# Twenty instead of twenty-three weight pieces converted early, late conversions that end on GpSimd, and a third buffer for q

## The chip, the cores and the metric

The kernel runs on one core of a Trainium2 chip. The metric is the device time of one execution in microseconds (us), lower is better. Three timed runs of the kernel before gave 1148.38, 1149.02 and 1145.77 us (median 1148.38). One further execution was recorded by the hardware profiler.

## The reference

```
# retention, 4 batches, 8 heads, 768 steps, head size 64
state = gamma * state + outer(k[t], v[t]);  y[t] = scale * q[t] @ state
x = y as 3072 tokens of 512
# first mixture: 8 experts, each takes 384 tokens
logits = x @ w_gate; walk all (token, expert) pairs in falling order of logit,
    give a free token to an expert that is not full
out[mask] = relu(x[mask] @ w1[e]) @ w2[e]
# second part, all tokens, width 1536
out = (sigmoid(x @ w_gate2) * (x @ w_val)) @ w_out
```

The three weights of the second part arrive as float64. [...]

## The kernel before

**Stages.** First comes the retention, in 24 iterations of 128 tokens: TensorE transposes q and k (`turn_q`, `turn_k`), multiplies (`stage_a`, `stage_y`), and turns the result back and takes the logits (`stage_x`), whose rows go to DRAM (`xd`). Then the routing of the first expert (`members(0)`), which has little beside it. Then eight experts in turn. An expert has two phases. In the first, `h_step` and `y_step` alternate over 8 blocks of the hidden width. In the second, `g_step` and `o_step` go over 12 blocks of the second part. Each product is made of three matmuls on a high and a low part of both factors: ScalarE rounds the high part (L584), VectorE subtracts to get the low part (L585), six pieces at most ahead of their use.

**Hooks.** Behind each product of an expert stands a hook (`hook()`), numbered from 0 (`units`); the first expert has 51. A hook does two things: it runs the next step of the routing of the following expert (small VectorE instructions, then compares `cm` at L255 and counting matmuls at L264 that read them), and it runs whatever the table `late` has at that number.

**The conversion of a piece.** The 36 pieces (128 rows by 512 numbers) of the three float64 weights end in the tile `wall`. For one piece: a DMA brings `raw`; ScalarE scales the low word (L151); VectorE shifts and masks the high word (L152) and joins sign and top bit (L154); ScalarE takes the absolute value of the high word (L156), GpSimd adds the low word (L157); VectorE multiplies by the test "not smaller than the smallest normal" (L159). Before, 23 pieces are converted in slots of the retention (`conv_at`, two slots per iteration) and 13 in hooks of the first expert (`LATE`, three hooks for each piece: L151, L152 and L154 in hook u, L156 and L157 in u+1, L159 in u+3).

**Order.** The schedule is written by hand: each engine executes its instructions in the order in which the program issues them. SyncE issues nearly all DMAs, in program order too; it waits at a DMA whose buffer is still in use, with everything behind it. GpSimd also scales k in the retention (L277) and issues the indirect gathers and scatters of tokens.

Of the kernel before, what the change touches and what calls it, by code (L numbers as in the profile page):

```python
# [8 lines left out]
F32 = mybir.dt.float32  # L9
# [5 lines left out]
OP = mybir.AluOpType  # L15
# [4 lines left out]
def retention_moe_glu_kernel(  # L20
# [15 lines left out]
    PE, ACT, DVE, POOL, SP = nc.tensor, nc.scalar, nc.vector, nc.gpsimd, nc.sync  # L36
    B, H, S, D = q.shape
    C = S // 128
    NCH = B * C
# [20 lines left out]
    loads = attn.enter_context(tc.tile_pool(name="loads", bufs=5))  # L60
# [6 lines left out]
    tq, tk, tv = {}, {}, {}  # L67

    def load_q(j):
        b, g = divmod(j, C // 2)  # L70
        tq[j] = loads.tile([128, H, 2, D], F32, name="q", bufs=2)
        SP.dma_start(tq[j].rearrange("p h r d -> p h (r d)"),
                     q[b, :, g * 256:(g + 1) * 256, :].rearrange("h (p r) d -> p h (r d)", r=2))

    def load_k(i):
        b, c = divmod(i, C)
        tk[i] = loads.tile([128, H, D], F32, name="k", bufs=6)
        SP.dma_start(tk[i], k[b, :, c * 128:(c + 1) * 128, :].rearrange("h t d -> t h d"))

    def load_v(i):  # L80
        b, c = divmod(i, C)
        tv[i] = loads.tile([128, H, D], F32, name="v", bufs=5)
        SP.dma_start(tv[i], v[b, :, c * 128:(c + 1) * 128, :].rearrange("h t d -> t h d"))
# [9 lines left out]
    load_k(0)  # L93
    load_k(1)
    load_q(1)
    load_v(0)
    load_k(2)
# [28 lines left out]
    SMALLEST = 1.125 * 2.0 ** -15  # L126
# [18 lines left out]
    def conv_steps(m):  # L145

        t = raws.pop(m)
        lo, hi = t[:, :, 0], t[:, :, 1]
        w = wall[:, seq[m]].rearrange("p a b -> p (a b)")
        wi = w.bitcast(I32)  # L150
        ACT.activation(lo, lo.bitcast(U32), AF.Copy, scale=2.0 ** -29)  # L151
        DVE.tensor_scalar(wi, hi, 3, 0x3FFFFFFF, op0=OP.logical_shift_left, op1=OP.bitwise_and)  # L152
        yield
        DVE.scalar_tensor_tensor(wi, hi, -1073741824, wi, op0=OP.bitwise_and, op1=OP.bitwise_or)  # L154
        yield
        ACT.activation(hi.bitcast(F32), hi.bitcast(F32), AF.Abs)  # L156
        POOL.tensor_tensor(wi, wi, lo, OP.add)  # L157
        yield
        DVE.scalar_tensor_tensor(w, hi.bitcast(F32), SMALLEST, w, op0=OP.is_ge, op1=OP.mult)  # L159

    steps = {}

# [106 lines left out]
    def scale_q(j):  # L269
        raw = tq[j]  # L270
        tq[j] = work.tile([128, 2, H, D], F32, name="qs", bufs=2)
        for r in range(2):
            DVE.tensor_tensor(tq[j][:, r], raw[:, :, r, :],
                              dq[:, j % (C // 2), r, :, None].to_broadcast([128, H, D]), OP.mult)

    def scale_k(i):
        POOL.tensor_tensor(tk[i], tk[i], dk[:, i % C, :, None].to_broadcast([128, H, D]), OP.mult)  # L277

    def turn_q(u):
        j, z = divmod(u, 2)  # L280
        if z == 0:
            qT[j] = work.tile([128, HP, 256], F32, name="qT", bufs=3)
        p = psa.tile([128, 2, 128, 2], F32, name="pT", bufs=2)
        for a in range(2):
            for r in range(2):
                h = 4 * z + 2 * a
                PE.transpose(p[:, a, :, r], tq[j][:, r, h:h + 2, :], ident)
        ACT.activation(qT[j][:, 2 * z:2 * z + 2, :], p.rearrange("p a i r -> p a (i r)"), AF.Copy)

    def turn_k(i):  # L290
        p = psa.tile([128, HP, 128], F32, name="pT", bufs=2)
        for a in range(HP):
            PE.transpose(p[:, a, :], tk[i][:, 2 * a:2 * a + 2, :], ident)
        kT[i] = work.tile([128, HP, 128], F32, name="kT", bufs=3)
        ACT.activation(kT[i], p, AF.Copy)
# [4 lines left out]
    def stage_a(i):  # L300
        am = work.tile([128, 2, HP, 128], F32, name="am", bufs=2)
        ps = [psa.tile([128, HP, 128], F32, name=f"pA{s}") for s in range(2)]
        for a in range(HP):
            for s in range(2):
                r = slice(s * 64, (s + 1) * 64)
                PE.matmul(ps[s][:, a, :], kT[i][r, a, :], q_of(i)[r, a, :], start=True, stop=True)  # L306
        for s in range(2):
            DVE.tensor_tensor(am[:, s], ps[s], mask_b, OP.mult)
        AM[i] = am

    def stage_y(i):
        c = i % C
        pY = psa.tile([128, HP, 128], F32, name="pY")

        if c:
            for a in range(HP):
                PE.matmul(pY[:, a, :], Sbd[c % 2][:, a, :], q_of(i)[:, a, :], start=(a == 0), stop=False,  # L317
                          skip_group_check=True)
        for a in range(HP):
            for s in range(2):  # L320
                PE.matmul(pY[s * 64:(s + 1) * 64, a, :], tv[i][:, 2 * a + s, :], AM[i][:, s, a, :],  # L321
                          start=(not c and a == 0), stop=True, skip_group_check=True)
        t = work.tile([128, HP, 128], F32, name="xT", bufs=2)
        ACT.activation(t, pY, AF.Copy)
        XT[i] = t
        if c < C - 1:
            for a in range(HP):
                PE.matmul(pS[:, a, :], tk[i][:, 2 * a:2 * a + 2, :], tv[i][:, 2 * a:2 * a + 2, :],  # L328
                          start=(c == 0 and a == 0), stop=(c == C - 2), skip_group_check=True)
            sn = Sbd[(c + 1) % 2]  # L330
            for s in range(2):
                r = slice(s * 64, (s + 1) * 64)
                ACT.activation(sn[r, :, r], pS[r, :, r], AF.Copy)

    def stage_x(i):
        xs = work.tile([128, HP, 128 + E], F32, name="xs", bufs=3)
        for z in range(2):
            p = psa.tile([128, 2, 128 + E], F32, name=f"pX{z}")
            for a in range(2):
                PE.matmul(p[:, a, :], XT[i][:, 2 * z + a, :], eyew[:, 2 * z + a, :], start=True, stop=True)  # L340
            if z:
                ACT.activation(xs[:, 2:, :], p, AF.Copy)
            else:
                DVE.tensor_copy(xs[:, :2, :], p)
        SP.dma_start(xd[i * 128:(i + 1) * 128, :].rearrange("p (a b) -> p a b", a=HP), xs[:, :, :128])
        XS[i] = xs
# [21 lines left out]
        DVE.tensor_reduce(lg[:, i, :], XS[i][:, :, 128:].rearrange("p a e -> p e a"), AX, OP.add)  # L368


    EARLY = 23
    LATE = [1 + 5 * n // 2 for n in range(NP - EARLY)]
    RAWS = 3
    conv_at = {4 + n * 41 // EARLY: n for n in range(EARLY)}

    def conv_slot(u):
        if u + 3 in conv_at:
            conv_load(conv_at[u + 3], conv, 5)
        if u in conv_at:
            conv_step(conv_at[u], 2)  # L380
        if u - 1 in conv_at:
            conv_step(conv_at[u - 1])
        if u - 3 in conv_at:
            conv_step(conv_at[u - 3])

    for i in range(NCH):
        if i + 5 < NCH:
            load_k(i + 5)
        if i + 4 < NCH:
            load_v(i + 4)  # L390
        if i % 2 == 0 and i // 2 + 3 < NCH // 2:
            load_q(i // 2 + 3)
        if i % 2 == 0 and i // 2 + 2 < NCH // 2:
            scale_q(i // 2 + 2)
        if i + 3 < NCH:
            scale_k(i + 3)
        if i + 2 < NCH:
            turn_k(i + 2)
        if i + 3 < NCH:
            turn_q(i + 3)  # L400
        if i + 1 < NCH:
            stage_a(i + 1)
        conv_slot(2 * i)
        stage_y(i)
        if i:
            stage_x(i - 1)
        if i >= 2:
            reduce_x(i - 2)
        conv_slot(2 * i + 1)
        if i == 1:  # L410
            late_consts()
        if i == NCH - 4:
            prep_tiles()
            prep(0, 10, True)
        if i == NCH - 3:
            begun = [compare(0, 0, 10, 1 << widths[0], r["edb"], OP.is_le)]
        if i == NCH - 2:
            prep(10, 20, True)
            begun.append(compare(1, 10, 20, 1 << widths[0], r["edb"], OP.is_le))
# [9 lines left out]
    main = ctx.enter_context(tc.tile_pool(name="main", bufs=1))  # L429
# [30 lines left out]
    def fetch_tokens(x):  # L460
# [11 lines left out]
        if x == 0:  # L472
            for n in range(RAWS):
                conv_load(EARLY + n, main, RAWS)

# [275 lines left out]
    late = {}  # L751
    for n, u in enumerate(LATE):
        m = EARLY + n
        if n + RAWS < len(LATE):
            late.setdefault(u + 4, []).append((conv_load, m + RAWS, main, RAWS))
        late.setdefault(u, []).append((conv_step, m, 2))
        late.setdefault(u + 1, []).append((conv_step, m))
        late.setdefault(u + 3, []).append((conv_step, m))

    for x in range(E):  # L760
        job[0] = members(x + 1) if x + 1 < E else None
# [67 lines left out]
```

## Time and profile before

| | |
|---|---|
| median of three runs | 1148.38 us |
| profiled execution, its own time | 1153.54 us |
| span of that execution, first to last instruction | 1151.7 us |
| TensorE busy | 1129.8 us |
| VectorE busy | 704.5 us |
| ScalarE busy | 489.1 us |
| GpSimd busy | 135.4 us |

A busy TensorE is no sign that it is at its peak: its matmuls overlap, and at a granted clock of half speed it is just as busy. The profile has to be read stage by stage. The retention ends at about 162 us and the products of the first expert run from about 195 to 321 us. In the names, PE is TensorE, PEld its weight loads, DVE VectorE, ACT ScalarE, POOL GpSimd, SP SyncE.

### The profile page before, as it was taken

How to read it: one execution, taken by the hardware profiler on the slowest of the kernel's cores; microseconds unless marked ns; L12 is line 12 of the kernel's file. 1: busy time of each engine (PE TensorE's matmuls, PEld its weight loads, DVE VectorE, ACT ScalarE, POOL GpSimd, SP SyncE). 2: the span in 40 equal slices, each digit the busy share in tenths (PEclk: the TensorE clock that was granted, in tenths of full speed). 3: DMA queues.
4: the chain of work that ended last, by engine and by line, in shares of the span. 5: the costliest groups of instructions: out<-in, count | busy, mean ns of one | idle time of the engine just before them, and what ended most of it. 6: DMA issues, size and time to landing. Idle time of an engine off the chain costs nothing.

```text
span 1151.7 us, 18988 instructions
## 1 busy us (share of the span) xinstructions
PE 1129.8 (98%) x7502; PEld 1052.5 (91%) x7502; DVE 704.5 (61%) x1577; ACT 489.1 (42%) x954; POOL 135.4 (12%) x147
## 2 busy tenths in 40 slices
PE   8999998999999999999999999999999999999997
PEld 6998886999999999999999999999999999999996
DVE  3877874988566646565656656565665545554543
ACT  2665631555443344334433443334343444443442
POOL 3444511222110001001100110010001010101001
PEclk8998997999999999999999999999999999999999
DMA  9999915224010201021100310030103020301000
GB/s 212 249 257 260 272 54 192 91 83 159 27 65 1 110 28 65 1 91 47 65 2 17 122 55 11 1 138 10 55 1 137 1 65 17 121 10 56 1 1 28
DMA packets 109609, 91.47 MB, mean 79 GB/s; under 512 B 54736, under 2 KB 92624, under 8 KB 109520
## 3 DMA queue, kind: packets, MB, share of 16 engines
q1 hardware_dynamic: 105680, 77.67, 23.1%
q0 software_dynamic: 3840, 12.59, 3.4%
q8 instruction: 59, 0.97, 0.3%
q14 instruction: 30, 0.25, 0.1%
HBM read 77.66 MB, written 12.58 MB: 78 GB/s over the span
## 4 chain that ended last, share of the span: by engine, by line
PE 82%; issue 10%; DVE 3%; DMA 2%; SPq 2%; POOL 1%; ACT 0%; POOLq 0%; DVEq 0%; ACTq 0%
PE mm L646 14%; PE mm L648 13%; PE mm L647 13%; PE pr L264 5%; PE acc L706 5%; PE acc L707 5%; PE acc L708 5%; PE acc L646 3%; PE acc L648 3%; PE acc L647 3%; PE pA L306 2%; PE pY L321 2%; PE pY L317 2%; PE pS L328 2%; PE pX L340 2%
## 5 line engine op out<-in xcount | busy, mean ns | idle before, releaser
L646 PE MATMUL mm<-x2T,piece 128*128 128x384 f32 x768 | 260.8, 340 | 0.0
L648 PE MATMUL mm<-x2T,piece 128*128 128x384 f32 x768 | 257.7, 336 | 0.0
L647 PE MATMUL mm<-x2T,piece 128*128 128x384 f32 x768 | 257.0, 335 | 0.0
L585 DVE TENSOR_TENSOR piece<-wall,piece 128x512 fp32r<-128x512 f32 x288 | 185.9, 686 | 0.0
L584 ACT ACTIVATE piece<-wall 128x512 fp32r<-128x512 f32 x288 | 163.0, 617 | 0.0
L584 ACT ACTIVATE gT<-gv 128x384 fp32r<-128x384 f32 x96 | 50.5, 526 | 243.2 <-DVE gv L690 241.0
L690 DVE TENSOR_TENSOR gv<-mm,sg 128x384 f32<-128x384 f32 x96 | 53.3, 555 | 155.6 <-PE mm L648 153.2
L646 PEld LDWEIGHTS mm<-x2T,piece 128*128 128x128 f32 x768 | 144.9, 189 | 3.1
L647 PEld LDWEIGHTS mm<-x2T,piece 128*128 128x128 f32 x768 | 144.3, 188 | 2.8
L648 PEld LDWEIGHTS mm<-x2T,piece 128*128 128x128 f32 x768 | 144.1, 188 | 0.0
L706 PE MATMUL acc<-piece,gT 128*128 128x512 f32 x288 | 115.3, 400 | 0.0
L707 PE MATMUL acc<-piece,gT 128*128 128x512 f32 x288 | 113.6, 394 | 0.0
L708 PE MATMUL acc<-piece,gT 128*128 128x512 f32 x288 | 113.6, 394 | 0.0
L688 ACT ACTIVATE sg<-mm 128x384 f32<-128x384 f32 x96 | 46.9, 488 | 125.2 <-PE mm L648 122.1
L658 ACT ACTIVATE hT<-mm 128x384 fp32r<-128x384 f32 x64 | 31.5, 491 | 159.5 <-PE mm L648 131.4
L659 DVE SCALAR_TENSOR_TENSOR hT<-mm,hT 128x384 fp32r<-128x384 f32 x64 | 35.6, 557 | 103.3 <-ACT hT L658 101.7
L585 DVE TENSOR_TENSOR gT<-gv,gT 128x384 fp32r<-128x384 f32 x96 | 54.1, 563 | 56.8 <-ACT gT L584 56.8
L646 PE MATMUL acc<-hT,piece 128*128 128x384 f32 x256 | 88.5, 346 | 0.0
L646 PE MATMUL mm<-xT,piece 128*128 128x384 f32 x256 | 86.7, 339 | 0.7 <-ACT xT L584 0.7
L648 PE MATMUL mm<-xT,piece 128*128 128x384 f32 x256 | 86.6, 338 | 0.0
L647 PE MATMUL mm<-xT,piece 128*128 128x384 f32 x256 | 86.4, 337 | 0.0
L648 PE MATMUL acc<-hT,piece 128*128 128x384 f32 x256 | 86.3, 337 | 0.0
(139 smaller groups left out, 1861.0 us busy)
## 6 DMA issues: line engine op xcount, KB each, us to landing
w2s<-in_moe_w_dram SPq DMA_DIRECT2D x64, 256.0 KB, 6.6
w1s<-in_moe_w_dram SPq DMA_DIRECT2D x7, 2048.0 KB, 7.7
q<-in_q_dram SPq DMA_DIRECT2D x12, 512.0 KB
k<-in_k_dram SPq DMA_DIRECT2D x24, 256.0 KB, 6.1
v<-in_v_dram SPq DMA_DIRECT2D x24, 256.0 KB, 5.6
raw<-in_moe_w_gate_dram SPq DMA_DIRECT2D x12, 512.0 KB, 6.8
raw<-in_moe_w_val_dram SPq DMA_DIRECT2D x12, 512.0 KB, 5.0
xd<-xs SPq DMA_DIRECT2D x24, 256.0 KB, 4.5
```

Of the source, the lines that this page charges most:

```text
L264: PE.matmul(pr, cm[:, :, c - c0], rhs(c), start=(c == 0), stop=(c == NCH - 1))
L584: ACT.activation(hi, src, AF.Copy)
L585: eng.tensor_tensor(lo, src, hi.bitcast(F32), OP.subtract)
L646: PE.matmul(p, w[:, 0, dt, :], r[0], start=start, stop=False)
L647: PE.matmul(p, w[:, 1, dt, :], r[0], start=False, stop=False)
L648: PE.matmul(p, w[:, 0, dt, :], r[1], start=False, stop=stop)
L659: DVE.scalar_tensor_tensor(t[:, 1], p, 0.0, t[:, 0].bitcast(F32), op0=OP.max, op1=OP.subtract)
L688: ACT.activation(sg, p, AF.Sigmoid)
L690: DVE.tensor_tensor(gv, ps[1], sg, OP.mult)
L706: PE.matmul(p, gT[g][:, 0, r], w[:, 0], start=(g == 0), stop=False)
L707: PE.matmul(p, gT[g][:, 0, r], w[:, 1], start=False, stop=False)
L708: PE.matmul(p, gT[g][:, 1, r], w[:, 0], start=False, stop=(g == GB - 1))
```

## The change

Twenty pieces are converted in the retention, at most one per iteration, and sixteen in the first expert. Those sixteen have no L159 on VectorE: right behind the add, GpSimd makes the test (a `tensor_scalar` on `raw`) and multiplies by it. The hooks of a late piece go from three to two, and the load into its buffer is issued one hook later. The tile q gets a third buffer, and from the fourth on it is loaded one iteration earlier.

```
-        tq[j] = loads.tile([128, H, 2, D], F32, name="q", bufs=2)
+        tq[j] = loads.tile([128, H, 2, D], F32, name="q", bufs=3)
...
         POOL.tensor_tensor(wi, wi, lo, OP.add)
-        yield
-        DVE.scalar_tensor_tensor(w, hi.bitcast(F32), SMALLEST, w, op0=OP.is_ge, op1=OP.mult)
+        if m < EARLY:
+            yield
+        h = hi.bitcast(F32)
+        if m < EARLY:
+            DVE.scalar_tensor_tensor(w, h, SMALLEST, w, op0=OP.is_ge, op1=OP.mult)
+        else:
+            POOL.tensor_scalar(h, h, SMALLEST, None, op0=OP.is_ge)
+            POOL.tensor_tensor(w, w, h, OP.mult)
...
-    EARLY = 23
+    EARLY = 20
-    conv_at = {4 + n * 41 // EARLY: n for n in range(EARLY)}
+    conv_at = {4 + n * 42 // EARLY: n for n in range(EARLY)}
...
-        if i % 2 == 0 and i // 2 + 3 < NCH // 2:
-            load_q(i // 2 + 3)
+        if (i % 2 or i == 0) and (i + 1) // 2 + 3 < NCH // 2:
+            load_q((i + 1) // 2 + 3)
...
-            late.setdefault(u + 4, []).append((conv_load, m + RAWS, main, RAWS))
+            late.setdefault(u + 5, []).append((conv_load, m + RAWS, main, RAWS))
         late.setdefault(u, []).append((conv_step, m, 2))
         late.setdefault(u + 1, []).append((conv_step, m))
-        late.setdefault(u + 3, []).append((conv_step, m))
```

On GpSimd, from the last pieces of the retention over the first gathers (`xg`) into the first expert, before:

```order
L277 TENSOR_TENSOR k<-k,dk 128x512
L157 TENSOR_TENSOR wall<-wall,raw 128x512 x3
L434 DMA xg<-xd,idx 128x512 x3
L467 MEMSET w1s 128x4
L157 TENSOR_TENSOR wall<-wall,raw 128x512 x12
L434 DMA xg<-xd,idx 128x512 x3
L157 TENSOR_TENSOR wall<-wall,raw 128x512
L716 MEMSET spacer 1x1
```

and the same place now (L164 is the test, L165 the multiplication):

```order
L157 TENSOR_TENSOR wall<-wall,raw 128x512 x3
L440 DMA xg<-xd,idx 128x512 x3
L473 MEMSET w1s 128x4
L157 TENSOR_TENSOR wall<-wall,raw 128x512
L164 TENSOR_SCALAR raw<-raw 128x512
L165 TENSOR_TENSOR wall<-wall,raw 128x512
L157 TENSOR_TENSOR wall<-wall,raw 128x512
L164 TENSOR_SCALAR raw<-raw 128x512
L165 TENSOR_TENSOR wall<-wall,raw 128x512
```

Each late piece now puts three instructions in a row into GpSimd's queue where one stood; twelve such groups stand ahead of the second expert's gathers and four behind them.

On VectorE, in the first phase of the first expert (`hT` is the hidden block's low part, `fl` the flag behind a routing count), before:

```order
L659 SCALAR_TENSOR_TENSOR hT<-mm,hT 128x384
L585 TENSOR_TENSOR piece<-w2s,piece 128x512
L159 SCALAR_TENSOR_TENSOR wall<-raw,wall 128x512
L585 TENSOR_TENSOR piece<-w1s,piece 128x512
L659 SCALAR_TENSOR_TENSOR hT<-mm,hT 128x384
L585 TENSOR_TENSOR piece<-w2s,piece 128x512
L159 SCALAR_TENSOR_TENSOR wall<-raw,wall 128x512
L152 TENSOR_SCALAR wall<-raw 128x512
L154 SCALAR_TENSOR_TENSOR wall<-raw,wall 128x512
L512 TENSOR_SCALAR fl,fb<-pr 128x8
```

and now, with line numbers six higher:

```order
L665 SCALAR_TENSOR_TENSOR hT<-mm,hT 128x384
L591 TENSOR_TENSOR piece<-w2s,piece 128x512
L591 TENSOR_TENSOR piece<-w1s,piece 128x512
L665 SCALAR_TENSOR_TENSOR hT<-mm,hT 128x384
L591 TENSOR_TENSOR piece<-w2s,piece 128x512
L152 TENSOR_SCALAR wall<-raw 128x512
L154 SCALAR_TENSOR_TENSOR wall<-raw,wall 128x512
L518 TENSOR_SCALAR fl,fb<-pr 128x8
```

Two L159 are gone from this stretch, and nothing else of it moved.

In SyncE's queue, at the second and third iteration of the retention, before:

```order
L72 DMA q<-in_q_dram 128x8x128
L139 DMA raw<-in_moe_w_gate_dram 128x4x256
L78 DMA k<-in_k_dram 128x8x64
L83 DMA v<-in_v_dram 128x8x64
L139 DMA raw<-in_moe_w_val_dram 128x4x256
L345 DMA xd<-xs 512x1x128
L78 DMA k<-in_k_dram 128x8x64
L83 DMA v<-in_v_dram 128x8x64
L72 DMA q<-in_q_dram 128x8x128
```

and now:

```order
L72 DMA q<-in_q_dram 128x8x128
L139 DMA raw<-in_moe_w_gate_dram 128x4x256
L78 DMA k<-in_k_dram 128x8x64
L83 DMA v<-in_v_dram 128x8x64
L72 DMA q<-in_q_dram 128x8x128
L351 DMA xd<-xs 512x1x128
L139 DMA raw<-in_moe_w_val_dram 128x4x256
L78 DMA k<-in_k_dram 128x8x64
L83 DMA v<-in_v_dram 128x8x64
```

The second q of the loop has taken the place of the second raw load, which now stands behind the first store of `xd`.

## Rows read from the trace of the kernel before

**Rows 1.** Windows, retention: length, busy PE, PEld, DVE, ACT, POOL, clock, DMA, GB/s.

```profile
90.00:100.00 10.00, 8.35 (x72) 7.01 (x69) 9.00 (x14) 6.06 (x12) 3.78 (x3) 0.85 1.08 268
100.00:110.00 10.00, 10.00 (x91) 8.86 (x91) 6.09 (x10) 4.79 (x10) 3.67 (x3) 0.81 0.92 247
```

**Rows 2.** Timeline, TensorE, retention: start, us, instruction [idle before <-releaser].

```profile
93.51 0.60 PE L293 MATMUL pT<-ident,k 128*128 128x128 f32 x4
...
96.50 2.67 PE L306 MATMUL pA<-qT,kT 64*128 64x128 f32 x16
...
104.35 1.09 PE L340 MATMUL pX<-eyew,xT 128*128 128x136 f32 x8
105.28 0.60 PE L293 MATMUL pT<-ident,k 128*128 128x128 f32 x4
...
106.24 1.16 PE L306 MATMUL pA<-qT,kT 64*128 64x128 f32 x16
...
110.44 1.09 PE L340 MATMUL pX<-eyew,xT 128*128 128x136 f32 x8
```

**Rows 3.** Timeline, VectorE, the same place.

```profile
90.93 0.43 DVE L152 TENSOR_SCALAR wall<-raw 128x512 int32<-128x512 int32 x1 [2.13 <-DMA raw<-in_moe_w_gate_dram]
...
92.60 3.24 DVE L273 TENSOR_TENSOR qs<-q,dq 128x512 f32<-128x512 f32 x2
```

**Rows 4.** Timeline, GpSimd, the same place.

```profile
92.22 1.63 POOL L157 TENSOR_TENSOR wall<-wall,raw 128x512 int32<-128x512 int32 x1 [3.52 <-ACT kT L295]
93.80 1.49 POOL L277 TENSOR_TENSOR k<-k,dk 128x512 f32<-128x512 f32 x1
```

**Rows 5.** Waits of SyncE's queue on q buffers: us in total, times, longest.

```profile
SPq L72 <- DVE qs L273: 0.7, 1, 0.7
```

**Rows 6.** Windows, first expert (columns as in Rows 1).

```profile
205.00:225.00 20.00, 19.11 (x125) 18.41 (x123) 19.27 (x41) 10.69 (x21) 5.98 (x4) 1.00 0.24 79
225.00:295.00 70.00, 69.58 (x444) 64.74 (x445) 59.53 (x140) 36.87 (x70) 15.89 (x13) 0.98 0.34 117
```

**Rows 7.** Timeline, weight loads of TensorE, first expert.

```profile
225.38 0.76 PEld L264 LDWEIGHTS <-cm 128*128 128x128 bf16 x11 [1.21 <-DVE cm L255]
```

**Rows 8.** Timeline, GpSimd, first expert.

```profile
206.00 1.31 POOL L157 TENSOR_TENSOR wall<-wall,raw 128x512 int32<-128x512 int32 x1 [16.46 <-DVE wall L154]
...
220.04 1.74 POOL L157 TENSOR_TENSOR wall<-wall,raw 128x512 int32<-128x512 int32 x1 [6.60 <-issue]
223.52 1.31 POOL L157 TENSOR_TENSOR wall<-wall,raw 128x512 int32<-128x512 int32 x1 [1.74 <-DVE wall L154]
```

**Rows 9.** Timeline, VectorE, first and (last row) second expert.

```profile
206.16 1.19 DVE L231 TENSOR_SCALAR tmp<-m 128x24 int32<-128x24 int32 x1
...
221.02 0.56 DVE L659 SCALAR_TENSOR_TENSOR hT<-mm,hT 128x384 fp32r<-128x384 f32 x1 [0.43 <-ACT hT L658]
...
223.58 1.29 DVE L523 TENSOR_TENSOR edb<-ed,dig 128x24 bf16<-128x24 f32 x1
...
244.38 0.18 DVE L523 TENSOR_TENSOR edb<-ed,dig 128x24 bf16<-128x24 f32 x1
...
328.31 0.18 DVE L231 TENSOR_SCALAR tmp<-m 128x24 int32<-128x24 int32 x1
```

**Rows 10.** Instructions on tile raw: count, ns min/median/max, first and last start.

```profile
L152 DVE TENSOR_SCALAR wall<-raw x36: 408/418/1289, 35.1 to 283.9; 128x512 int32<-128x512 int32 x36
L154 DVE SCALAR_TENSOR_TENSOR wall<-raw,wall x36: 691/692/1415, 35.6 to 284.4; 128x512 int32<-128x512 int32 x36
L157 POOL TENSOR_TENSOR wall<-wall,raw x36: 1288/1318/1760, 36.4 to 290.0; 128x512 int32<-128x512 int32 x36
...
L159 DVE SCALAR_TENSOR_TENSOR wall<-raw,wall x36: 665/684/1511, 43.9 to 291.3; 128x512 f32<-128x512 f32 x36
```

**Rows 11.** Instructions of L277 (columns as in Rows 10).

```profile
L277 POOL TENSOR_TENSOR k<-k,dk x24: 1035/1046/1500, 7.7 to 139.2; 128x512 f32<-128x512 f32 x24
```

**Rows 12.** Groups by line, GpSimd: busy us, mean ns | idle before.

```profile
masks.py:199 POOL TENSOR_SCALAR_AFFINE_SELECT ident<-ident 128x128 f32<-128x128 f32 x1 | 0.3, 293 | 0.1
```

## Prediction

> **What bounds the kernel now.** I read the windows first, since the whole-span share of a busy TensorE says nothing, then the timelines of the stages that the change touches. In the retention TensorE goes from product to product, with one break. Two windows there are below full clock, 0.85 and 0.81 [rows 1]. From L293 to L306 it takes 106.24 - 105.28 = 0.96 us in an undisturbed iteration and 96.50 - 93.51 = 2.99 us at the break; from L306 to L340 it takes 110.44 - 106.24 = 4.20 us and 104.35 - 96.50 = 7.85 us [rows 2]. So the break costs 2.03 us of lateness and 3.65 us in a pass at half clock (1.2 instead of 2.4 GHz), 5.7 us in all. Its cause stands on VectorE: a conversion waited 2.13 us for its raw load, and q's scaling behind it took 3.24 us for two [rows 3], beside GpSimd's L157 and L277 [rows 4].
>
> In the first expert VectorE is the bound to begin with: busy 19.27 of the 20 us from 205 to 225 us, against 59.53 of the next 70 [rows 6]. At 225.38 us TensorE had waited 1.21 us for a compare [rows 7]; lateness of VectorE up to there passes to the end of the kernel in full. All later stages are untouched.
>
> **How the two engines share.** L231 starts at 206.16 beside L157 (206.00 to 207.31) and ends at 207.35, after 1.19 us; without GpSimd it takes 0.18 us. L523 starts at 223.58 beside L157 (223.52 to 224.83) and ends at 224.87; alone it takes 0.18 us [rows 8, 9]. So a VectorE instruction of this kind does not run slower: it stands until GpSimd's is over. Between two GpSimd instructions in a row VectorE gets one in: L277 behind L157 took 1.49 us instead of its median 1.05 [rows 4, 11], and the two scalings of q were held once each. An L659, which reads PSUM, ran its 0.56 us from 221.02 in the middle of an L157 (220.04 to 221.78) and was not held [rows 8, 9]. The instructions that fill VectorE here (piece, cm, L152, L154, the small routing ones) read SBUF alone.
>
> The Trainium skill (SBUF — State Buffer, section "Who interferes with whom") has this as an exclusive lock: a Vector instruction with two SBUF inputs, or in a two-port mode, and a GpSimd instruction that reads SBUF exclude each other for a whole instruction. The trace agrees (1.19 us instead of 0.18). The rule goes further than the rows in that it covers the new test with its single input; by it both new GpSimd instructions hold VectorE, without it only the multiplication would be sure to, and the first phase would cost 4 x 0.8 = 3.2 us less than the sum below says.
>
> **The change part by part.**
>
> *Three pieces fewer in the retention, one per iteration at most.* TensorE sets the pace there, so VectorE's, ScalarE's and GpSimd's saved instructions are worth nothing except at the break. The break came where two pieces fell into one iteration together with a scaling of q; no iteration has that now, and each raw load has the same lead as before with fewer bytes around it. Gain: 5.7 us at most, in the profiled execution. That execution took 1153.54 us, 5.2 us over the median of 1148.38, so the timed runs can hardly have had the whole break; one of them took 1145.77. For them I take half, -2.8 us, with bounds -5.7 and 0.
>
> *q with three buffers, loaded an iteration earlier.* SyncE waited for a q buffer once, 0.7 us [rows 5]; that is all that a buffer can give back at once. The load changes places with a raw load of the same size. Cost and gain: 0; if a raw load gets late by it instead, the bound is a break like the one above, +5.7 us.
>
> *L159 leaves VectorE in the first expert.* 13 instructions of 0.684 us [rows 10], 8.9 us of VectorE. Two of them lie ahead of 225 us, where VectorE is the bound: -1.4 us.
>
> *Test and multiplication on GpSimd, 16 times each.* No row has either. For the multiplication (two inputs, 128x512 float32) the nearest row is L277, same operation and type, median 1.05 us; L157, which reads the same strided raw, takes 1.32 [rows 10, 11]. I take 1.05. For the test (one input) the ends are 0.29 us, a one-input select on a quarter of the elements [rows 12], and 1.32. I take 0.8, nearer to L277, which has as many elements. Together 1.85 us, bounds 1.34 and 2.64.
>
> The Trainium skill (GPSIMD Engine Reference, section "4.1 Engine selection") calls two-input elementwise work on GpSimd about twice as slow as on VectorE and one-input work roughly line-rate; an estimate from that page is 2 x 0.68 for the multiplication and 0.4 to 0.7 for the test, 1.8 to 2.1 us, and the sum by it would be the same within 1 us.
>
> *First phase, 205 to 225 us.* Four L157 fall there [rows 6, 8], so four pairs of new instructions. VectorE has no idle time to put them in (0.43 us at 221.02 [rows 9] is the largest), and nearly all that it runs is of the held kind: 4 x 1.85 = 7.4 us of holds, less 1.4 us for two L159, is +6.0 us at the compare for which TensorE already waits. Bounds: with 2.64 us and every hold in full 4 x 2.64 - 1.4 = +9.2; with 1.34 us and half of it falling on L659 and other instructions that are not held 4 x 0.67 - 1.4 = +1.3.
>
> *Second phase, 225 to 295 us.* Here VectorE has 70 - 59.53 = 10.5 us idle [rows 6]. To come: 9 old pieces (POOL x13 there, less three gathers and a memset) and 3 new. Holds 12 x 1.85 = 22.2 us, of which about two thirds meet a held instruction (gv and the x2T products read PSUM, and there are waits): +14.8. The three new pieces bring L152 and L154, 3 x (0.42 + 0.69) = +3.3 [rows 10]. Eleven L159 go: -7.5. That is +10.6 against 10.5 us of cover; since pieces come in bunches and the cover doesn't, I take +1.5. Bounds 0 (more of it meets a wait) and +6 (nine tenths of the holds hit). ScalarE's three more L151 and L156 lie beside its idle time, 36.87 us busy of 70 [rows 6].
>
> *The queues.* SyncE's raw loads of the first expert now wait for GpSimd's multiplication instead of L159; GpSimd is done with a piece some 4 us behind L154 (1.32 + 1.85 us and a VectorE instruction or two between), which is no later than L159 two hooks further on. Behind GpSimd's new instructions stand the second expert's gathers, late by at most one group, 1.3 + 1.85 us. VectorE is past its full stretch by then, and I take nothing; +3 us is the bound.
>
> Sum: +6.0 + 1.5 - 2.8 = +4.7 us: 1148.38 + 4.7 = 1153.1 us. The profiled execution, which had the whole break, would go from 1153.54 by +7.5 - 5.7 to 1155.3.
>
> **Rivals.** *The holds are hidden by half.* For it: some VectorE instructions are not held, and before 225 us TensorE needed VectorE late only by 1.21 us. Against it: 19.27 of 20 us busy. Then the first expert costs 4 x 0.93 - 1.4 = 2.3 us and the second phase nothing, against -2.8: 1148 us, no change.
>
> *The first expert is relieved.* If the new instructions are short (1.34 us) and fall into VectorE's waits, the lost L159 win: the 1.21 us at the compare and the slow stretch behind it (clock 0.98 over 70 us, 1.4 us [rows 6]) go too, and the break is gone in every run: -5.7 - 2.6 = -8.3, 1140 us; with the retention's share alone 1143 us. For it: the break is in the only trace, and a pair of pieces in one iteration is what it had beside it. Against it: the timed runs are 5.2 us faster than that trace already.
>
> *The lock bites in both phases and TensorE's clock falls.* At 2.64 us a pair, +9.2 and +6, and each long idle of TensorE is followed by a slow stretch as that at 96.50 was (3.65 us more); this decides once VectorE is over 4 us late at a compare. With -2.8 and one such stretch: +16, 1164 us; halfway to it 1159.
>
> *The change doesn't do what it says:* the third buffer removes a wait of 0.7 us that ends nothing. It is in the sum as 0.
>
> **How the numbers follow.** A measurement of this kernel tells about 0.3% from no change, 3.4 us. The forecast (lock, first phase exposed, 1153.1 us, with its own range of 1150 to 1157) has 0.37, the lock in both phases with a falling clock 0.12, holds hidden by half 0.24, and the relieved first expert 0.27. Faster is the last one, 0.27; the same is holds hidden by half and the low edge of the forecast, 0.27; slower is the rest, 0.46. The range has to reach into the faster case and to the middle of the worst: 1143 to 1160 us.
>
> **What would show it.** Right: in the first expert rows of L152, L154, piece and cm of 1.5 us and more, a wait of TensorE on cm or hT of several us in the first phase, a second expert's first product later by about 8 us counted from the first gathers, and no break in the retention. The price shows in GpSimd's two new groups. Wrong: pairs of 1.3 us or less; VectorE with idle time before the second routing count; a break in the retention as before, which would leave +7.5 us and more; or a wait on raw in the first expert, which I do not expect.

## The result and the profile after

The changed kernel takes 1160.26 us (median of four runs, 1159.35 to 1160.92). Four runs of the kernel before, taken beside it, have a median of 1147.40 us (1145.77 to 1149.02). The ratio is 1.0114, with an interval of 1.0100 to 1.0128: 12.9 us slower, where +4.7 us was forecast. The profiled execution of the changed kernel took 1159.35 us, with a span of 1157.6 us.

The retention has no break any more. These are the windows of the kernel after that answer to [rows 1], with the same columns; the clock stands third from the end.

```profile
90.00:100.00 10.00, 10.00 (x111) 8.84 (x110) 7.89 (x15) 6.26 (x14) 5.58 (x4) 1.00 1.10 270
100.00:110.00 10.00, 10.00 (x105) 9.13 (x105) 7.15 (x15) 7.30 (x16) 3.63 (x4) 1.00 1.08 265
```

TensorE is busy for all of both windows, at full clock (1.00). What is lost is lost in the first expert. To see where, I cut it at three instructions that every version has: the first gather of the first expert's tokens (GpSimd L434, L440 after), the first product of the second phase (TensorE's weight load of `x2T`), and the first scatter of results (GpSimd L717, L723 after). In what follows, phase one runs from the gather to `x2T` and phase two from `x2T` to the scatter. From the scatter to the end every version takes 828.7 to 829.0 us, so nothing comes back later.

The span of the profiled execution of before contains a disturbed start, as the last experiment shows. For a comparison by phase I therefore use a second profile of the kernel before, unchanged (that experiment, b0). Its two phases as windows, columns as in [rows 1]:

```profile
180.95:232.26 51.31, 45.51 (x301) 42.80 (x300) 38.34 (x83) 24.12 (x46) 11.05 (x10) 0.93 0.47 150
232.26:316.76 84.50, 84.45 (x501) 78.02 (x500) 64.19 (x139) 42.99 (x81) 14.26 (x12) 1.00 0.26 88
```

The same two phases of the kernel after:

```profile
175.33:232.80 57.47, 49.02 (x301) 45.48 (x300) 42.33 (x75) 23.86 (x45) 26.58 (x19) 0.88 0.40 132
232.80:328.65 95.85, 87.32 (x501) 79.14 (x500) 81.08 (x139) 46.03 (x87) 53.99 (x38) 0.98 0.27 94
```

The first gather comes 180.95 - 175.33 = 5.6 us earlier; phase one is 57.47 - 51.31 = 6.2 us longer and phase two 95.85 - 84.50 = 11.4 us. Together that is +11.9 us, the difference of the two spans (1157.6 - 1145.7). The first pair of numbers in each row splits the loss further. Length less busy TensorE is the time in which TensorE had nothing: 5.80 us before and 8.45 after in phase one (+2.7), 0.05 and 8.53 in phase two (+8.5). The rest is TensorE being busy longer with the same instructions, +3.5 and +2.9 us; there the granted clock is lower (0.93 to 0.88, and 1.00 to 0.98). One profile of a phase is not exact: the first profile of the kernel before has 53.04 us in phase one, at a clock of 0.90, where b0 has 51.31; phase two is 84.50 us in both.

TensorE's idle times in the kernel after, from the timeline of its weight loads (in brackets the idle time before the instruction and what ended it), where before had [rows 7]:

```profile
200.67 0.19 PEld L654 LDWEIGHTS acc<-hT,piece 128*128 128x128 f32 x1 [1.45 <-DVE hT L665]
...
218.20 0.58 PEld L270 LDWEIGHTS <-cm 128*128 128x128 bf16 x8 [2.57 <-DVE cm L261]
...
234.47 0.19 PEld L654 LDWEIGHTS mm<-x2T,piece 128*128 128x128 f32 x1 [1.33 <-DVE x2T L591]
...
268.03 0.10 PEld L556 LDWEIGHTS <-after 128*128 128x128 bf16 x1 [2.60 <-issue]
...
276.24 0.19 PEld L712 LDWEIGHTS acc<-piece,gT 128*128 128x128 f32 x1 [1.99 <-ACT piece L590]
...
309.00 0.42 PEld L599 LDWEIGHTS mm<-ident,xg 128*128 128x128 f32 x4 [3.19 <-DVE xT L591]
```

Four of the six name VectorE: `hT`, the routing's compare `cm`, the low parts `x2T` and `xT`. The other two stand behind it. At 268.03 the matmul in front of that weight load waited 2.53 us for VectorE's scan `sc`; at 276.24 ScalarE had waited 5.42 us itself for VectorE's `gv`, which stood behind three `cm` of 3.00 us.

How VectorE comes to be late is seen around the second of them. GpSimd in the kernel after (start, us, instruction):

```profile
211.51 1.73 POOL L157 TENSOR_TENSOR wall<-wall,raw 128x512 int32<-128x512 int32 x1 [3.41 <-issue]
213.20 2.02 POOL L164 TENSOR_SCALAR raw<-raw 128x512 f32<-128x512 f32 x1
215.31 1.30 POOL L165 TENSOR_TENSOR wall<-wall,raw 128x512 f32<-128x512 f32 x1
216.58 1.28 POOL L157 TENSOR_TENSOR wall<-wall,raw 128x512 int32<-128x512 int32 x1
217.84 1.77 POOL L164 TENSOR_SCALAR raw<-raw 128x512 f32<-128x512 f32 x1
```

VectorE beside it:

```profile
213.71 0.86 DVE L152 TENSOR_SCALAR wall<-raw 128x512 int32<-128x512 int32 x1
214.61 0.69 DVE L154 SCALAR_TENSOR_TENSOR wall<-raw,wall 128x512 int32<-128x512 int32 x1
...
215.49 1.16 DVE L529 TENSOR_TENSOR edb<-ed,dig 128x24 bf16<-128x24 f32 x1
216.69 2.59 DVE L261 TENSOR_TENSOR cm<-iox,edb 128x512 bf16<-128x512 bf16 x3
```

`edb` ends at 216.65 with the L165 (216.61). The three `cm` then take 2.59 us beside the next two GpSimd instructions (1.09 us where nothing holds them, below); TensorE, which waits for the first of them, goes on at 218.20, after the L157 (217.86). What [rows 8, 9] showed for single L157 is now a chain of GpSimd instructions with hardly a gap. The members of the chain do not hold alike. The two-input ones, the add L157 and the multiplication L165, hold `cm` and `edb` to their ends. The test L164, with one input, lets instructions through: beside the one from 213.20 to 215.22, L152 takes 0.86 us instead of 0.42, and L154, with two inputs, runs from 214.61 in its usual 0.69 us.

The price of the two new instructions, from all instructions on the tile raw of the kernel after (ns min/median/max), beside [rows 10]:

```profile
L164 POOL TENSOR_SCALAR raw<-raw x16: 1555/1770/2070, 196.8 to 307.8; 128x512 f32<-128x512 f32 x16
L165 POOL TENSOR_TENSOR wall<-wall,raw x16: 1283/1327/1863, 198.6 to 309.9; 128x512 f32<-128x512 f32 x16
```

The test alone takes 1.56 us where VectorE does not stand in its way. The pair takes at least 1.56 + 1.28 = 2.84 us, and 1.77 + 1.33 = 3.10 by the medians.

Last, VectorE's groups in phase two of b0 (busy us, mean ns | idle before):

```profile
L585 DVE TENSOR_TENSOR piece<-wall,piece 128x512 fp32r<-128x512 f32 x32 | 20.5, 685 | 0.0
L585 DVE TENSOR_TENSOR gT<-gv,gT 128x384 fp32r<-128x384 f32 x12 | 7.2, 596 | 7.1 <-ACT gT L584 7.1
L690 DVE TENSOR_TENSOR gv<-mm,sg 128x384 f32<-128x384 f32 x12 | 6.7, 554 | 9.7 <-PE mm L648 7.3 <-PE mm L593 1.8 <-ACT sg L688 0.6
L159 DVE SCALAR_TENSOR_TENSOR wall<-raw,wall 128x512 f32<-128x512 f32 x9 | 6.1, 681 | 1.6 <-POOL spacer L716 1.6
L154 DVE SCALAR_TENSOR_TENSOR wall<-raw,wall 128x512 int32<-128x512 int32 x7 | 4.8, 693 | 0.2
L152 DVE TENSOR_SCALAR wall<-raw 128x512 int32<-128x512 int32 x7 | 2.9, 418 | 0.0
```

The same groups after:

```profile
L591 DVE TENSOR_TENSOR piece<-wall,piece 128x512 fp32r<-128x512 f32 x33 | 30.1, 953 | 0.1
L154 DVE SCALAR_TENSOR_TENSOR wall<-raw,wall 128x512 int32<-128x512 int32 x11 | 10.6, 962 | 0.4
L591 DVE TENSOR_TENSOR gT<-gv,gT 128x384 fp32r<-128x384 f32 x12 | 7.4, 620 | 7.2 <-ACT gT L590 7.2
L152 DVE TENSOR_SCALAR wall<-raw 128x512 int32<-128x512 int32 x11 | 7.1, 647 | 0.0
L696 DVE TENSOR_TENSOR gv<-mm,sg 128x384 f32<-128x384 f32 x12 | 6.6, 550 | 5.7 <-PE mm L654 4.5 <-ACT sg L694 1.1
```

Piece, L154 and L152 are each 230 to 270 ns longer in the mean; `gv`, which reads PSUM (the memory that TensorE writes), is not, and `gT` hardly is (24 ns). The idle time in front of `gT` is as long as before, 7.2 us. Here VectorE waits for ScalarE to round the `gv` that VectorE has just written. That wait comes back in each of the 12 blocks with 16.9 us more work on VectorE as without it, so it covered nothing.

### The profile page after: what moved, and what is told of

Same layout as the page of the kernel before. It is cut to its first block, busy times and chain, and to the rows that moved or that the text cites. A ratio compares the mean times of both kernels' runs of the same rounds, so it can differ in the third digit from the quotient of the medians.

```text
span 1157.6 us, 19016 instructions
## 1 busy us (share of the span) xinstructions
PE 1127.2 (97%) x7502; PEld 1048.8 (91%) x7502; DVE 719.8 (62%) x1561; ACT 488.2 (42%) x954; POOL 185.5 (16%) x179
## 4 chain that ended last, share of the span: by engine, by line
PE 77%; issue 10%; DVE 8%; ACT 1%; DMA 1%; SPq 1%; POOL 1%; POOLq 0%; DVEq 0%; ACTq 0%
PE mm L652 12%; PE mm L654 12%; PE mm L653 12%; PE pr L270 5%; PE acc L712 5%; PE acc L714 5%; PE acc L713 5%; PE acc L652 3%; PE acc L654 3%; PE acc L653 3%; DVE piece L591 2%; PE pA L312 2%; PE pY L327 2%; PE pX L346 2%; PE pS L334 2%
## 5 line engine op out<-in xcount | busy, mean ns | idle before, releaser
L591 DVE TENSOR_TENSOR piece<-wall,piece 128x512 fp32r<-128x512 f32 x288 | 194.8, 717 | 0.1
L440 POOL DMA_INDIRECT xg<-xd,idx x24 | 24.4, 1018 | 479.5 <-issue 446.4
L652 PE MATMUL mm<-xT,piece 128*128 128x384 f32 x256 | 86.9, 339 | 0.7 <-ACT xT L590 0.7
L654 PE MATMUL mm<-xT,piece 128*128 128x384 f32 x256 | 86.7, 339 | 0.0
```

Source lines behind the costliest of these rows:

```text
L591: eng.tensor_tensor(lo, src, hi.bitcast(F32), OP.subtract)
L652: PE.matmul(p, w[:, 0, dt, :], r[0], start=start, stop=False)
L654: PE.matmul(p, w[:, 0, dt, :], r[1], start=False, stop=stop)
```

## The experiments

**Two parts, apart.** a1 is the change without GpSimd's ending; a2 is that ending alone (with its two hooks and the later load), on the kernel before.

```
# a1: the change, but the late pieces end as before
-        tq[j] = loads.tile([128, H, 2, D], F32, name="q", bufs=2)
+        tq[j] = loads.tile([128, H, 2, D], F32, name="q", bufs=3)
-    EARLY = 23
+    EARLY = 20
-    conv_at = {4 + n * 41 // EARLY: n for n in range(EARLY)}
+    conv_at = {4 + n * 42 // EARLY: n for n in range(EARLY)}
...
# a2: before, with EARLY = 23, q with two buffers, and
+        if m < EARLY:
+            DVE.scalar_tensor_tensor(w, h, SMALLEST, w, op0=OP.is_ge, op1=OP.mult)
+        else:
+            POOL.tensor_scalar(h, h, SMALLEST, None, op0=OP.is_ge)
+            POOL.tensor_tensor(w, w, h, OP.mult)
```

> Twenty pieces early and q with three buffers as in the change, but the sixteen late pieces end on VectorE (L159) in a third hook, and their loads are issued one hook earlier, as before. Theory (GpSimd's two new instructions hold VectorE, and the rest of the change is cheap): the first expert loses its excess of some 16 us but for three more pieces (3 x 1.8 us of VectorE, mostly in idle time, +1 to +3 us), the retention keeps its gain of 3 to 4 us; 1144 to 1149 us. Rival (three more pieces in the first expert, with their loads, are the cost, wherever they end): 1156 us or more.

> The kernel before with one part of the change: its thirteen late pieces end on GpSimd (two hooks, load one hook later). Theory: most of the loss comes back, the first phase as in the change (+6 us), the second phase less than in the change because no pieces bunch up behind the gathers of the second expert; +8 to +13 us, 1155 to 1160 us. Rival (the three more pieces are the cost): within 3 us of before.

Measured: a1 1144.19 us (ten runs, 1142.09 to 1146.07), ratio to before 0.9977 (0.9966 to 0.9988). a2 1158.86 us (four runs, 1155.38 to 1160.69), ratio 1.0094 (1.0067 to 1.0121). The phases of a1:

```profile
178.24:229.92 51.68, 46.98 (x302) 44.23 (x301) 38.51 (x83) 24.29 (x47) 11.10 (x10) 0.90 0.47 149
229.92:315.60 85.68, 85.16 (x501) 77.98 (x500) 71.67 (x148) 46.19 (x87) 18.86 (x16) 1.00 0.32 105
```

The phases of a2:

```profile
182.51:238.89 56.38, 48.68 (x302) 45.16 (x300) 42.47 (x76) 23.82 (x45) 26.48 (x19) 0.91 0.42 133
238.89:330.00 91.11, 86.72 (x501) 79.63 (x500) 70.55 (x133) 43.22 (x81) 38.91 (x28) 0.98 0.24 81
```

So the whole loss is the ending on GpSimd: 12.5 us over before with 13 pieces, 1160.26 - 1144.19 = 16.1 us over a1 with 16. (The kernel after was timed beside a kernel before of 1147.40 us, the runs here beside one of 1146.36; with each taken from its own, the 16.1 are 15.0.) The other parts gain: a1 does the full work and is 2.2 us under before. The rows hold a second lesson. In phase two VectorE is busy 71.67 us in a1 and TensorE has 85.68 - 85.16 = 0.5 us idle; in a2 VectorE is busy less, 70.55 us, and TensorE has 4.4 us idle. So the sum of VectorE's work does not decide. TensorE's waits above point to where it stands: in front of `cm`, `hT` and `gv`, for which TensorE or ScalarE waits. No run moves work to another place and keeps its sum.

**q alone.** The kernel before with q's third buffer and earlier load, nothing else.

> The kernel before with a third buffer for q and its load one iteration earlier, nothing else. Theory (q's buffer was no wait that ended anything): within 2 us of before. Rival (the retention's gain of the changed kernel comes from q): -3 us or more.

Measured: 1144.68 us (ten runs, 1143.17 to 1149.06), ratio 0.9989 (0.9973 to 1.0004): not told apart from before by the times. Its trace says more, with that of b0 beside it. VectorE at the break in b0:

```profile
88.36 0.43 DVE L152 TENSOR_SCALAR wall<-raw 128x512 int32<-128x512 int32 x1 [3.50 <-DMA raw<-in_moe_w_gate_dram]
...
90.03 3.23 DVE L273 TENSOR_TENSOR qs<-q,dq 128x512 f32<-128x512 f32 x2
```

And in a3:

```profile
86.19 0.43 DVE L152 TENSOR_SCALAR wall<-raw 128x512 int32<-128x512 int32 x1 [0.79 <-DMA raw<-in_moe_w_gate_dram]
```

With q out of its way the raw load arrives 2.2 us earlier; the scaling of q behind it is held as before, and the first gather comes at 178.77 instead of 180.95 us. So q's part of the profiled gain is 2.2 us, and the three pieces fewer give the rest: with them the first gather comes at 175.22 to 175.77 us in the four profiles whose start runs at full clock (after, a4, b1, b4).

**No ending at all.** As after, without test and multiplication for the late pieces: this takes away what GpSimd runs and leaves all else.

```
         else:
-            POOL.tensor_scalar(h, h, SMALLEST, None, op0=OP.is_ge)
-            POOL.tensor_tensor(w, w, h, OP.mult)
+            pass
```

> The changed kernel without the test and the multiplication of the sixteen late pieces: numbers under the smallest normal are not set to zero there. Theory: without the two instructions GpSimd holds VectorE only for the add, and VectorE has no L159 either; the first expert is then shorter than that of the kernel before, 1140 to 1145 us. Rival (the pieces' other instructions, loads and hooks cost): 1150 us or more.

Measured: 1143.82 us (ten runs, 1140.55 to 1146.23), ratio 0.9976 (0.9964 to 0.9988). Its phases:

```profile
175.77:228.12 52.35, 47.19 (x302) 44.54 (x301) 35.87 (x79) 24.22 (x46) 11.07 (x10) 0.90 0.46 150
228.12:312.67 84.55, 84.48 (x501) 77.95 (x500) 63.91 (x136) 46.28 (x87) 17.27 (x16) 1.00 0.29 100
```

Phase two is that of before. Phase one is 1.0 us longer than in b0, so the first expert is not shorter than before, though I had expected it to be; the gain is the retention's. The two instructions cost 1160.26 - 1143.82 = 16.4 us (15.4 with each kernel taken from the kernel before timed beside it), and the hooks, loads and sixteen pieces around them about 1 us by the phases. a1, which does the same work on VectorE, is within 0.4 us of a4: L159 on VectorE cost nothing that these times can tell.

**Held, or only late?** The pair could hurt by holding VectorE, or by delivering the pieces late because GpSimd is busy. b1 puts two fills of the dead `raw` in its place, which take as long (1.56 and 1.30 us) and read nothing.

```
-            POOL.tensor_scalar(h, h, SMALLEST, None, op0=OP.is_ge)
-            POOL.tensor_tensor(w, w, h, OP.mult)
+            scratch = t.rearrange("p a c -> p (a c)").bitcast(BF)
+            POOL.memset(scratch[:, :1760], 0.0)
+            POOL.memset(scratch[:, :1440], 0.0)
```

> The changed kernel with the two new GpSimd instructions of each late piece replaced by two fills of the raw tile (1760 and 1440 two-byte numbers, about as long: 1.3 to 1.6 us each by the fill of 1280 at 1.16 us); small numbers are not set to zero in the late pieces. The fills read nothing. Theory (GpSimd's reading holds VectorE's instructions with two SBUF inputs): GpSimd is as long busy, yet pieces, cm and L154 run free and only the single-input ones (L152, small routing ones) are held; 1144 to 1150 us. Rival (GpSimd's queue is late, whatever it does, and raw buffers and gathers wait for it): within 3 us of the changed kernel, 1157 us or more.

Measured: 1153.29 us (four runs, 1151.41 to 1154.23), ratio 1.0064 (1.0044 to 1.0085), between the two theories. Its phases:

```profile
175.63:231.16 55.53, 47.88 (x301) 44.49 (x300) 38.55 (x76) 24.09 (x45) 25.08 (x19) 0.91 0.41 134
231.16:322.19 91.03, 86.49 (x501) 78.86 (x500) 74.50 (x138) 46.23 (x87) 50.26 (x37) 0.98 0.29 99
```

GpSimd of b1 at the place shown above for after:

```profile
217.68 1.30 POOL L157 TENSOR_TENSOR wall<-wall,raw 128x512 int32<-128x512 int32 x1 [1.32 <-ACT piece L591]
219.04 1.56 POOL L165 MEMSET raw<- 128x1760 bf16 x1
220.66 1.30 POOL L166 MEMSET raw<- 128x1440 bf16 x1
```

VectorE of b1 beside it:

```profile
217.73 1.29 DVE L530 TENSOR_TENSOR edb<-ed,dig 128x24 bf16<-128x24 f32 x1
219.05 1.09 DVE L262 TENSOR_TENSOR cm<-iox,edb 128x512 bf16<-128x512 bf16 x3
...
220.67 1.32 DVE L254 TENSOR_SCALAR dig<-di 128x24 f32<-128x24 int32 x1
```

Beside L157 `edb` is held (1.29 us). Beside a fill the three `cm` run freely, 1.09 us instead of 2.59. But `dig`, with one input, stands through the whole second fill (to 221.99; the fill ends at 221.96), and the pieces behind it stand with it. The Trainium skill (SBUF — State Buffer, section "Who interferes with whom") has both: a two-input VectorE instruction contends only with a GpSimd instruction that reads SBUF, while `copy`, `cast` and `tensor_scalar` can enter a two-port mode, which contends with GpSimd. The trace agrees, with 0.36 us for each `cm` and 1.32 us for `dig`. It does not agree that a GpSimd instruction that reads always locks a two-input one out for its whole length: the test, which reads `raw`, had L154 run beside it in its usual 0.69 us. So 16.4 us splits: 1153.29 - 1143.82 = 9.5 us need no reading by GpSimd (one-input instructions held, and pieces that come late: TensorE waits 2.77 us for one at 273.70), and 6 to 7 us more come when GpSimd reads.

**The test alone.** As after, without the multiplication: each piece has one new GpSimd instruction instead of two.

> The changed kernel with the test on GpSimd but without the multiplication; small numbers are not set to zero in the late pieces. Theory (holds add up by GpSimd's busy time; the test is 1.57 of 2.9 us of a pair, and without both the kernel takes 1143.8 us, with both 1160.3): 1150 to 1154 us. Rival (the test, with its one input, does not hold VectorE): 1143 to 1147 us.

Measured: 1148.23 us (ten runs, 1146.67 to 1150.22), ratio 1.0013 (1.0001 to 1.0025), under what I expected and just above the rival. Its phases:

```profile
178.18:232.86 54.68, 48.64 (x301) 45.54 (x300) 38.26 (x78) 24.18 (x46) 18.99 (x14) 0.88 0.44 145
232.86:319.78 86.92, 85.17 (x501) 77.93 (x500) 69.68 (x136) 46.42 (x87) 37.28 (x26) 1.00 0.30 100
```

The test, 1.6 to 1.8 us of the pair's 3, costs 1148.23 - 1143.82 = 4.4 us; the multiplication on top of it costs 12.0 (11.0 with each kernel taken from its own before). In phase two the idle time of TensorE grows from 0.07 us (a4) to 1.75 (test) and 8.53 (both). So the price does not follow GpSimd's busy time, and the windows of a4, b5 and after, with the same VectorE instructions to within one, show a reason. Over both phases the test adds 27.9 us of busy GpSimd and 8.2 us of busy VectorE; the multiplication adds 24.3 us and 15.5 us. The test holds VectorE for less of its length, as the rows of after showed. Per microsecond of holds the multiplication is still dearer, 12.0 for 15.5 us against 4.4 for 8.2; that the first holds fall into VectorE's waits would explain it, but no run shows that apart.

**Which pieces.** b4 ends the first six late pieces on GpSimd and the last ten on VectorE, b3 the other way round.

```
# b4; in b3 each condition is m < EARLY + 6
-        if m < EARLY:
+        if m < EARLY or m >= EARLY + 6:
             yield
...
+        if m < EARLY or m >= EARLY + 6:
+            late.setdefault(u + 3, []).append((conv_step, m))
```

> The reverse: the first six late pieces end on GpSimd, the last ten on VectorE. Theory: +6 us over the kernel with all ends on VectorE (1144 us), 1148 to 1152 us. Rival (only the first phase exposes holds): 1157 us or more, as the changed kernel.

> The changed kernel with the first six late pieces (hooks 1 to 13) ending on VectorE as before, the last ten on GpSimd. Theory (two places, each with its own loss: +6 us in the first phase, +10 us in the second): the first phase is as before, the second still has its loss; 1151 to 1156 us. Rival (only VectorE's full stretch before 225 us exposes holds): 1144 to 1148 us.

Measured: b4 1152.29 us (1150.40 to 1153.46), ratio 1.0061 (1.0043 to 1.0078); b3 1156.92 us (1151.71 to 1157.94), ratio 1.0085 (1.0054 to 1.0116), four runs each. Both lie just above what I expected, by 0.3 and 0.9 us. The phases of b4:

```profile
175.22:232.68 57.46, 48.90 (x301) 45.36 (x300) 42.32 (x75) 23.82 (x45) 26.59 (x19) 0.88 0.41 133
232.68:319.89 87.21, 85.45 (x501) 77.98 (x500) 73.43 (x149) 46.52 (x87) 22.03 (x18) 1.00 0.31 103
```

The phases of b3:

```profile
176.73:230.08 53.35, 48.44 (x302) 45.62 (x301) 38.48 (x83) 24.24 (x46) 11.12 (x10) 0.87 0.45 146
230.08:326.39 96.31, 88.96 (x501) 80.37 (x500) 80.66 (x138) 45.89 (x87) 50.64 (x35) 0.96 0.28 93
```

b4 has the first phase of after to 0.01 us (57.46), and its second, 87.2 us, is far nearer to a1's 85.7 than to after's 95.9. b3 is the reverse: its first phase, 53.4 us, is near a1's 51.7, its second that of after (96.31 against 95.85). So each phase is lost by the pieces that end in it, and the larger loss is the second. The times do not add up, though: b4 is 8.1 us over a1 and b3 12.7, together 20.8 us, against 16.1 for all sixteen. By the profiles 1.5 us of this lie in b4's second phase and 1.7 us in b3's first; why is not shown.

**The kernel before, profiled again.** Unchanged, to see whether the break belongs to the kernel or to one execution.

> The kernel before, unchanged, profiled a second time. If the break of 5.7 us in the retention is a property of one execution (or of the transfers as they happened to come), this profile has the first gathers of expert 0 earlier than 185.46 us, by up to 8 us, and a shorter break or none, although q still has two buffers. If the break belongs to the two buffers of q, it stands again: VectorE and GpSimd late around 90 us, first gathers within 2 us of 185.46. Time 1144 to 1150 us, from gathers to scatter 137 to 138 us in both.

Measured: 1147.57 us for the execution, span 1145.7 us. The break stands again, at the same place and with the same cause (the two VectorE rows above), and it stood in a2 too, which has the same retention. But the first gather comes at 180.95 us, 4.5 us earlier than in the first profile, and from there to the scatter it takes 135.8 us and not the 137 to 138 that I had expected; phase one is the shorter one (51.31 against 53.04 us). The 4.5 us arise at the start, in the window from 10 to 30 us. The kernel before, first profile:

```profile
10.00:30.00 20.00, 16.57 (x140) 13.96 (x138) 6.27 (x10) 5.95 (x12) 8.12 (x11) 0.83 1.13 234
```

The second profile:

```profile
10.00:30.00 20.00, 17.62 (x181) 14.84 (x181) 10.05 (x20) 8.63 (x17) 7.92 (x11) 1.00 1.11 224
```

140 matmuls at a clock of 0.83 against 181 at full clock. What made the first profile long was this, not the break. What sets it off was not pursued; a1, b3 and b5 have a clock of 0.91 between 20 and 40 us, and their first gathers come at 178.24, 176.73 and 178.18 us.

## Why the prediction was wrong

The direction held, and the mechanism in the main: GpSimd's new instructions hold VectorE, TensorE then waits at `hT`, `cm` and behind the gathers of the second expert, and the break in the retention is gone. The test holds less of its length than the sum took for it. The size failed, +12.9 us measured against +4.7, and the outcome lies just above the range. By the forecast's own steps:

**Second phase, +1.5: the step that failed.** Measured +11.4 us. Its form was "+10.6 against 10.5 us of cover", work on VectorE against VectorE's idle time. With the rows of VectorE above, the work that came was 81.08 - 64.19 = 16.9 us. Of the 6.3 us more than forecast, 3.1 are holds: 16.9 + 6.1 (nine L159 gone) - 4.4 (four more L152 and L154) - 0.7 (one more piece) = 17.9 us, forecast 14.8. Another 1.4 us are L159 that I had counted there, nine and not eleven, and 1.8 us are a fourth converted piece and one more subtraction that fall behind `x2T`. Of the 16.9 us, 8.5 came out as idle time of TensorE and 8.4 were covered, where the sum had let 9.1 of 10.6 be covered. So 6.3 us more work and 0.7 us less cover make the 7.0 us by which 8.5 exceeds +1.5. The form failed too, since no balance of sums gives the loss: a2 with 70.55 us of busy VectorE loses 4.4 us of TensorE here, b4 with 73.43 loses 1.8. One of the waits, 3.19 us at 309.00, stands in the four groups behind the second expert's gathers. The step on the queues had put nothing there, with +3 us as its bound; a2, with one group in that place, has no such wait. And TensorE's slow stretches add 2.9 us, which the sum put at nothing.

**Pair price, 1.85 us with bounds 1.34 to 2.64.** It is at least 2.84 us, above the upper bound. The multiplication (1.28 to 1.33 us) was within its rows, nearer to L157 than to L277. The test failed: 1.56 us alone, and I had taken L157's 1.32 for its upper end, on the idea that one input can't cost more than two. I leaned on the select [rows 12], a quarter of the elements at 0.29 us; scaled by elements that is 1.2 us, and it does not read `raw`. The price alone does not mend the sum: with 3.10 us a pair it would give 4 x 3.10 - 1.4 = +11.0 us in the first phase, where 6.2 were measured; the sum also let each pair hold VectorE for all of its length, and the test does not. The Trainium skill (GPSIMD Engine Reference, section "4.1 Engine selection") calls one-input work roughly line-rate on GpSimd; here the trace does not agree, 1.56 us against 0.42 for VectorE's one-input L152, which reads the same strided tile. The estimate from that page, up to 2.1 us a pair, was still 0.7 us under the least measured. And by the sum's own form it would have added 12 x 0.25 x 2/3 = 2.0 us of holds in the second phase, so "the same within 1 us" held for the first phase alone.

**First phase, +6.0.** Measured +6.2 us, but the agreement is partly luck (from the first profile of before, which the sum was read from, it is 57.47 - 53.04 = +4.4). The sum was lateness of VectorE alone; TensorE's idle time grew by 2.7 us, and 3.5 us are a slower TensorE, the larger part of it in the slow stretch behind the 2.57 us of waiting. Busy VectorE grew by 42.33 - 38.34 = 4.0 us although four L159 and one converted piece left the phase (3.8 us): 7.8 us of holds for five pairs of at least 2.84, so about half of the pairs' time was held, not all of it. A price too low and a share too high made nearly the right number.

**Retention, -2.8.** By the profiles it is 5.6 us (b0 to after); by the times it is smaller: a1 is 2.2 us under before, with 1.6 us more spent in its first expert than in b0, so some 4 us. My reason for halving the break, that the timed runs could hardly have had it, was wrong: that profile was long by its start (4.5 us) and its first phase (1.7 us), and the break is in every profile of that retention. *q: 0* failed too, in the good direction: 2.2 us in the profile, since the raw load that it changes places with comes earlier, not only q.

**The rivals.** Nearest was the lock in both phases with a falling clock (0.12, halfway 1159): +6.2 and +11.4 us with slow stretches in both. Its condition, a compare over 4 us late, stood on no row, and the forecast's own +6.0 us at the compare met it; so a slow stretch belonged into the sum, which had none. TensorE's wait was shorter than that: 2.57 us of idle time before 218.20 were followed by a slow stretch from 219.94 to 225.85, 5.9 us in which TensorE's weight loads took 0.33 instead of 0.19 us. Nor is the length of the wait all: behind nearly the same wait of 1.2 us the first profile of before has a slow stretch [rows 6] and b0 has none. The rival with half-hidden holds falls with the measured loss, the one with a relieved first expert with the pair's price.

What stays open: how the 9.5 us of b1 divide between one-input instructions that are held and pieces that come late, and why a reading one-input GpSimd instruction lets VectorE through. No run separates the former or explains the latter.

## What to carry to other kernels

Work moved to an engine that shares a path with the busy one is not moved: sixteen L159 of 0.68 us were free on VectorE, and the same work on GpSimd cost 15 to 16 us. Ask of each instruction that is to be moved how much of its length it holds the other engine, one by one; here the multiplication cost more than the longer test. Count a cover in the places where a chain runs through the engine and not over the stage; waits that come back in each block (here 7.2 us before `gT`) take up nothing, and where work and cover are nearly equal the range of the forecast has to hold an error in either. Before a profile is set against a median, look for what made that execution long; here it was the start and one slow stretch, and the break that I discounted was real.

## What the runs showed of the hardware

- A `tensor_scalar` with one float32 input on GpSimd took 1.56 us at the least for 128x512 numbers at a stride of 8 bytes, more than a two-input `tensor_tensor` that reads the same tile (1.28 us).
- A fill on GpSimd, which reads nothing, left two-input VectorE instructions alone (0.36 us for a `cm`) and held a one-input one to its end (1.32 us for 128x24 numbers).
- GpSimd's two-input instructions held `edb` and `cm` to their ends (1.16 us for an `edb` of 0.18). The one-input test let VectorE through: sixteen tests added 27.9 us of busy GpSimd and 8.2 us of busy VectorE, sixteen multiplications 24.3 and 15.5 us.
- GpSimd is held too: beside a busy VectorE the test takes 1.77 us in the median and up to 2.07, against 1.56 at the least.
- Two GpSimd instructions per piece cost 16.4 us, the first of them alone 4.4.
